# Attention and gated FFN on one core: part of q and k converted by GpSimd's requests, the prologue's steps in another order

## The chip, the cores and the metric

The kernel runs on one core of a Trainium2 chip. The metric is the device time of one execution in microseconds. Before the change it is 343.33 us, the median of three runs (343.06 to 343.74).

## The reference

Inputs are q, k, v of shape 8 x 8 x 576 x 64 (batch, heads, sequence, head dimension) and three weight matrices, all float32.

```
scores = q @ k^T / sqrt(64)                 for each batch and head
scores += slope[h] * (-|i - j|)             slope[h] = 2 ** (-8 (h + 1) / 8)
kept only where 0 <= i - j < 128            (a causal window of 128 positions)
attn = exp(scores - max) / (sum + 1e-9)
x    = (attn @ v), heads side by side       4608 tokens x 512
out  = (gelu(x @ w_gate) * (x @ w_val)) @ w_out      w_gate, w_val 512 x 1536, w_out 1536 x 512
```

## The kernel before

The work goes batch by batch through attention and in groups of 512 tokens through the gated network. Attention of the next batches is woven into the network of the present group, so that TensorE is fed all the time. The schedule is written out by hand: each engine executes its instructions in the order of the program text, and waits are set by the data.

The change touches only the prologue, where nothing can be woven in yet: batch 0's first 384 positions have to go through the whole attention before the first matmul of the network can run.

Heads are handled in pairs, c = 0 to 3, two heads on the two halves of the 128 partitions. The prologue does this:

- **Requests (L650).** q and k of positions 0 to 383 come as float32 in eight requests of two heads each (192 KB, 256 runs of 768 bytes): seven from the queue of SyncE (SP), one (k of pair 0) from ScalarE's. They land in a piece of `wo` and of `qs[1]`, `ks[1]` that is not yet used (`raw`). GpSimd's queue brings, cast to bf16 on the way, the remaining rows 384 to 575 of q and k (`load_runs(0, 1, 0, 8)`, into `vb[1]`), v of batch 0 (`load_v`), and the first columns of the weights (`load_w`, each call one request for gate and one for value).
- **Constants (L654 to L690).** GpSimd makes a ramp `tmpl`; VectorE makes the identity, the distances `dist` with the window in them (`far`), and `slopes`, identity matrices scaled by each head's slope, which add the bias to the scores by a matmul (`biases0`, L284). ScalarE makes `emask`, the exponential of the decays, used for the rows after 384 (`decays`, L684).
- **Cast, transpose, arrange.** `cast` (L693) converts one pair's q or k to bf16 on VectorE or ScalarE; `first` (L708) transposes it on TensorE; `untangle` (L151) copies it from PSUM into `qT`, `kT` in the order of positions.
- **Scores.** `scores0` adds q k^T to the bias in PSUM (L199) and ScalarE takes the exponential (L204, 512 wide, two per pair).
- **Sums and inverses.** `products` (L435) sums the exponentials with a matrix of ones (`sums_first`), two pairs at a time; ScalarE takes the logarithm of the sums (L510) and the exponential of its negative (L511), which is the inverse. A matmul that has to follow another into the same bank waits through a relay on SP (L192).
- **Values.** `products` forms attn @ v, and `scale_first` (L514) multiplies with the inverses into `xT`.
- **Remaining rows.** `rest` (L719) transposes rows 384 to 575 of q and k, after a VectorE copy (L765) has rearranged them; four `untangle` copies follow. `scores0_rest` computes their scores, ScalarE their exponentials (L204, 384 wide, eight of them), VectorE the masks (L207).
- **First network steps.** `gate_val` (L557) multiplies `xT` with the weights; Gelu is on ScalarE (L563, with a table load before the first), the product with the value half on VectorE (L564).

PSUM has eight banks, taken in turn by `bank()`: a bank is free again when its last reader is done. The prologue's order before is the text at L727 to L805.

Of the kernel before, what the change touches and what calls it, by code (L numbers as in the profile page):

```python
# [7 lines left out]
FP32 = mybir.dt.float32  # L8
# [19 lines left out]
def kernel(  # L28
# [10 lines left out]
    nc = tc.nc  # L39
# [583 lines left out]
    def out_last(g):  # L623
        for lo in (0, 256):
# [16 lines left out]
    raw = [[wo[:, 3 + 3 * w:6 + 3 * w, :].rearrange("p a x -> p (a x)").bitcast(FP32),  # L641
            t[1].rearrange("p j x -> p (j x)")[:, 0:1536].bitcast(FP32)]
           for w, t in ((0, qs), (1, ks))]

    pairs0 = [t[0].rearrange("p j x -> p (j x)")[:, 0:1536].rearrange(
        "p (x c y) -> p x c y", x=3, c=4) for t in (qs, ks)]
    pairs1 = wo[:, 9:12, :]
    for h in (0, 2, 4, 6):
        for w, src in ((0, q), (1, k)):
            (nc.scalar if w and h == 0 else nc.sync).dma_start(  # L650
                out=raw[w][h // 4].rearrange("p (h x) -> p h x", h=4)[:, h % 4:h % 4 + 2, :],
                in_=src[0][h:h + 2, 0:384, :].rearrange("h (p r) d -> p h (r d)", r=3))

    nc.gpsimd.iota(tmpl, pattern=[[1, 256]], base=0, channel_multiplier=-1,  # L654
                   allow_small_or_imprecise_dtypes=True)
    nc.gpsimd.memset(ones64, 1.0)
    for t in kT + qT:
        nc.gpsimd.memset(t[:, :, 576:640], 0.0)
    for t in vb:
        nc.gpsimd.memset(t[64:128, 4, :], 0.0)  # L660
    load_runs(0, 1, 0, 8)
    load_v(0, (0, 1, 2))
    load_w(0, 128)
    load_w(128, 256)
    load_v(0, (3, 4))
    load_w(256, 512)

    for h in range(H):
        nc.vector.memset(slope1[:, h:h + 1], -8.0 * 2.0 ** (-8.0 * (h + 1) / H))
    nc.vector.memset(ones8, 0.0)  # L670
    nc.vector.memset(ones8.rearrange("p (h x) -> p h x", x=40)[:, :, 0:8], 1.0)
    nc.vector.tensor_single_scalar(out=ident, in_=tmpl[:, 0:128], scalar=0.0, op=ALU.is_equal)
# [3 lines left out]
    for x in (0, 1):  # L676
        half, to = slice(64 * x, 64 * x + 64), slice(64 * x, 64 * x + 192)
        nc.vector.tensor_tensor(out=dist[half, 0:192], in0=tmpl[half, to], in1=far[half, to], op=ALU.max)
    for to, n in ((192, 192), (384, 128)):
        nc.vector.tensor_copy(out=dist[:, to:to + n], in_=dist[:, 0:n])  # L680
# [11 lines left out]
    def cast(w, c, copy):  # L692
        copy(out=pairs0[w][:, :, c, :].rearrange("p x (i d) -> p x i d", i=2),  # L693
             in_=raw[w][c // 2].rearrange("p (c i x d) -> p c x i d", c=2, i=2, x=3)[:, c % 2])

    made_slopes(0, 4)

# [7 lines left out]
    def first(w, c, copy, ps):  # L705
        ps = ps.bitcast(BF16)
        for x in range(3):
            nc.tensor.transpose(out=ps[:, 128 * x:128 * x + 128], in_=pairs0[w][:, x, c, :],  # L708
                                identity=ident)
        untangle(copy, 0, 0, w, c, c + 1, ps)  # L710

    def rest(copies):
        pss = [bank().bitcast(BF16) for _ in range(2)]
        for c in (0, 2):
            for w, ps in enumerate(pss):
                p = 64 * w
                for n in (c, c + 1):
                    for x in range(3):
                        nc.tensor.transpose(  # L719
                            out=ps[:, 192 * n + 64 * x:192 * n + 64 * x + 64],  # L720
                            in_=pairs1[p:p + 64, x, 128 * n:128 * n + 128],
                            identity=ident[p:p + 64, p:p + 64])
        for c in (0, 2):
            for w, ps in enumerate(pss):
                untangle(copies[w], 0, 1, w, c, c + 2, ps[:, 192 * c:768])

    nc.scalar.preload_act_table_set("natural_log_exp_and_others")  # L727
    held = [bank(), bank()]
    keep_busy(held[0], 2, 128)
    keep_busy(held[0], 60)  # L730
    decays(0, 2)
    cast(0, 0, dve)
    cast(1, 0, act)
    made_slopes(4, 8)
    decays(2, 4)
    first(0, 0, dve, held[0])
    first(1, 0, act, held[1])
    cast(0, 1, dve)
    cast(1, 1, act)
    decays(4, 5)  # L740

    def pair(c, copies, between=None):
        held = [bank(), bank()]
        for w in (0, 1):
            first(w, c, copies[w], held[w])
            if w == 0 and between:
                between()

    cast(0, 2, dve)
    cast(1, 2, dve)  # L750
    scores0((0,), biases0((0,), 4), lambda: pair(1, (dve, act)))
    cast(1, 3, act)
    biases = biases0((1,))
    pair(2, (dve, dve), lambda: cast(0, 3, dve))
    scores0((1,), biases)
    biases = biases0((2,))
    pair(3, (dve, dve))
    scores0((2,), biases)
    scores0((3,), biases0((3,)))
    row(0)  # L760
    sums_a = products(0, sums_first(0))
    for step in zip(*(inverse_first(0, x, sums_a[x]) for x in (0, 1))):
        for do in step:
            do()
    dve(out=pairs1.rearrange("p x (h d) -> p h x d", d=64),  # L765
        in_=vb[1].rearrange("p j x -> p (j x)")[:, 0:1536].rearrange(
            "p (h x d) -> p h x d", h=H, x=3))
# [13 lines left out]
    rest((dve, dve))  # L781
    sums_b = products(0, sums_first(2))
    for x in (0, 1):
        ln, minus = inverse_first(2, x, sums_b[x])
        ln()
        decays(5 + x, 6 + x)
        minus()
    decays(7, 8)
    vals = products(0, values_first(0) + values_first(2, 2))
    for x in (0, 1):  # L790
        for c in (0, 2):
            scale_first(c, x, vals[c + x])
# [31 lines left out]

# [106 lines left out]
```

The softmax here doesn't subtract the row's maximum and nothing guards it: scores larger than these inputs give would overflow.

## Time and profile before

| what | value |
|---|---|
| runs | 343.06, 343.33, 343.74 us |
| span of the profiled execution | 342.5 us (0.8 below the median; what lies around the span is not in the profile) |
| granted TensorE clock | 1.000 over the span |
| TensorE busy | 331.1 us (97%) |
| VectorE, ScalarE, GpSimd busy | 190.8 (56%), 174.4 (51%), 108.1 us (32%) |
| software queue (GpSimd) q0 | 107424 packets, 18.10 MB |
| hardware queues q1 (SP), q10 (ScalarE) | 39104 and 3172 packets |
| first wide matmuls of the network (f = 2) | from 22.82 us on |

Times of the profile count from the start of the span. A line of the chain of waits has a start, a length and the engine and line that the end of the kernel hung on then; a line of the timeline has a start, a busy time, engine, line, operation, tiles, a count, and in brackets the idle time just before and what ended it. "PEld" is the weight load of TensorE, "SPq" the sequencer of SyncE. Beside these views the trace has a record of every DMA packet (queue, start, bytes) and of each request's sixteen partial landings.

### The profile page before, as it was taken

How to read it: one execution, taken by the hardware profiler on the slowest of the kernel's cores; microseconds unless marked ns; L12 is line 12 of the kernel's file. 1: busy time of each engine (PE TensorE's matmuls, PEld its weight loads, DVE VectorE, ACT ScalarE, POOL GpSimd, SP SyncE). 2: the span in 40 equal slices, each digit the busy share in tenths (PEclk: the TensorE clock that was granted, in tenths of full speed). 3: DMA queues.
4: the chain of work that ended last, by engine and by line, in shares of the span. 5: the costliest groups of instructions: out<-in, count | busy, mean ns of one | idle time of the engine just before them, and what ended most of it. 6: DMA issues, size and time to landing. Idle time of an engine off the chain costs nothing.

```text
span 342.5 us, 8046 instructions
## 1 busy us (share of the span) xinstructions
PE 331.1 (97%) x3268; PEld 170.1 (50%) x3310; DVE 190.8 (56%) x331; ACT 174.4 (51%) x339; POOL 108.1 (32%) x147
## 2 busy tenths in 40 slices
PE   7789999999999999999999999999999999999996
PEld 6467655444544454445444554445444544444443
DVE  8679564544599545944595369636773313303420
ACT  6884597536895338443753366344823133224322
POOL 9875663580094095008600680050000000000000
PEclk9999999999999999999999999999999999999999
DMA  8999999999599799979996999587114110020002
GB/s 202 169 196 190 204 164 146 143 188 170 132 145 175 125 190 190 191 165 98 182 183 121 121 181 185 133 107 103 63 40 100 64 64 0 0 94 31 0 31 95
DMA packets 149739, 43.49 MB, mean 127 GB/s; under 512 B 133541, under 2 KB 142661, under 8 KB 149701
## 3 DMA queue, kind: packets, MB, share of 16 engines
q0 software_dynamic: 107424, 18.10, 68.5%
q1 hardware_dynamic: 39104, 18.69, 22.3%
q10 hardware_dynamic: 3172, 6.19, 8.4%
q8 instruction: 26, 0.43, 0.5%
q14 instruction: 13, 0.10, 0.1%
HBM read 43.65 MB, written 9.53 MB: 155 GB/s over the span
## 4 chain that ended last, share of the span: by engine, by line
PE 87%; ACT 8%; DMA 2%; issue 1%; SPq 1%; DVE 0%; ACTq 0%
PE ps L557 54%; PE ps L593 22%; ACT P L204 5%; PE ps L435 4%; DMA ks<-in_k_dram 2%; PE ps L199 2%; PE ps L613 2%; PE ps L251 1%; PE ps L377 1%; ACT osb L598 1%; SPq L650 1%; PE ps L627 1%; PE ps L143 1%; ACT rb L511 0%; ACT rb L510 0%
## 5 line engine op out<-in xcount | busy, mean ns | idle before, releaser
L564 DVE TENSOR_TENSOR hT<-ps,gelu 128x512 bf16<-128x512 f32 (+3 forms) x119 | 74.2, 635 | 91.8 <-PE ps L557 77.8
L563 ACT ACTIVATE gelu<-ps 128x512 bf16<-128x512 f32 (+3 forms) x119 | 65.5, 558 | 103.4 <-PE ps L557 89.5
L557 PE MATMUL ps<-xT,wv 128*128 128x512 bf16 (+3 forms) x472 | 112.9, 359 | 0.4
L557 PE MATMUL ps<-xT,wg 128*128 128x512 bf16 (+3 forms) x461 | 111.7, 359 | 1.2 <-DVE xT L514 0.3
L593 PE MATMUL ps<-wo,hT 128*128 128x512 bf16 x376 | 88.2, 379 | 1.2 <-issue 0.5
L557 PEld LDWEIGHTS <-wv 128*128 128x128 bf16 x476 | 45.2, 98 | 48.6
L557 PEld LDWEIGHTS <-wg 128*128 128x128 bf16 x476 | 44.6, 98 | 48.7 <-issue 0.6
L204 ACT ACTIVATE P<-ps 128x384 bf16<-128x384 f32 (+2 forms) x128 | 55.9, 549 | 15.2 <-PE ps L199 15.0
L593 PEld LDWEIGHTS <-hT 128*128 128x128 bf16 x396 | 37.0, 98 | 44.1
L207 DVE TENSOR_TENSOR P<-P,emask 128x768 bf16<-128x768 bf16 (+1 forms) x60 | 34.4, 588 | 22.1 <-ACT P L204 21.2
L101 POOL DMA_DIRECT2D vb<-in_v_dram x40 | 34.0, 887 | 7.7 <-DMA ks<-in_k_dram 3.3
L598 ACT COPY osb<-ps 128x512 f32<-128x512 f32 x28 | 16.7, 596 | 35.6 <-PE ps L593 34.9
L101 POOL DMA_DIRECT2D qs<-in_q_dram x30 | 25.2, 858 | 5.8 <-DMA wo<-in_moe_w_out_dram 4.0
L882 POOL COPY mark<-hT 1x2 bf16<-1x2 bf16 x4 | 0.7, 174 | 79.6 <-DVE hT L564 79.6
L101 POOL DMA_DIRECT2D ks<-in_k_dram x30 | 25.4, 895 | 0.2 <-DMA qs<-in_q_dram 0.2
L492 DVE TENSOR_TENSOR xT<-ps,rb 128x512 bf16<-128x512 f32 (+3 forms) x29 | 14.3, 563 | 6.9 <-PE ps L435 6.9
L435 PE MATMUL ps<-P,vb 64*64 64x64 bf16 (+2 forms) x752 | 17.8, 221 | 0.3 <-SPq L192 0.2
L435 PEld LDWEIGHTS <-vb 64*64 64x64 bf16 x752 | 14.8, 107 | 4.3 <-issue 2.7
L331 DVE TENSOR_TENSOR T<-P 64x1024 bf16<-64x1024 bf16 (+1 forms) x20 | 15.0, 751 | 0.4
L199 PE MATMUL ps<-qT,kT 64*64 64x192 bf16 (+2 forms) x368 | 11.7, 236 | 0.1
L199 PEld LDWEIGHTS <-kT 64*64 64x64 bf16 x368 | 7.5, 106 | 6.2 <-issue 4.8
L468 DVE TENSOR_TENSOR xT<-ps,rb 128x512 bf16<-128x512 f32 (+1 forms) x10 | 6.4, 638 | 6.8 <-ACT rb L463 6.7
(88 smaller groups left out, 184.4 us busy)
## 6 DMA issues: line engine op xcount, KB each, us to landing
out_dram<-osb SPq DMA_DIRECT2D x35, 256.0 KB
rb<-rd ACTq DMA_DIRECT2D x10, 576.0 KB
vb<-in_v_dram POOLq DMA_DIRECT2D x32, 128.0 KB, 7.2
qs<-in_q_dram POOLq DMA_DIRECT2D x24, 128.0 KB, 4.9
ks<-in_k_dram POOLq DMA_DIRECT2D x24, 128.0 KB, 6.6
wo<-in_moe_w_out_dram POOLq DMA_DIRECT2D x2, 768.0 KB, 14.9
wg<-in_moe_w_gate_dram POOLq DMA_DIRECT2D x5, 256.0 KB, 8.4
wv<-in_moe_w_val_dram POOLq DMA_DIRECT2D x5, 256.0 KB, 9.0
```

Source lines behind the costliest of these rows:

```text
L101: nc.gpsimd.dma_start(out=t[0:n, j, :].rearrange("p (h d) -> p h d", h=H), in_=src[b][:, 128 * j:128 * j + n, :].rearrange("h p d -> p h d"))
L199: nc.tensor.matmul(out=out, lhsT=keys(b, c, m)[half, :], rhs=qT[b % 2][half, c, q0:q0 + n], start=first, stop=True, skip_group_check=not f ...
L204: nc.scalar.activation(out=dst, in_=src, func=AF.Exp, scale=0.125)
L207: nc.vector.tensor_tensor(out=dst, in0=dst, in1=m, op=ALU.mult)
L331: nc.vector.tensor_tensor(out=to[half, :, 2 * n0 + x:2 * n1 + x - 1:2], in0=P[half, :, 3 * n0:3 * n1 - 2:3], in1=P[half, :, 3 * n0 + 1:3 * ...
L435: mm = nc.tensor.matmul(out=out, lhsT=lhsT, rhs=prob(b)[half, c, i, col:col + q1 - q0], start=all(t[2] != u for t in todo[:n]), stop=True, ...
L492: nc.vector.tensor_tensor(out=xT[:, c, at:at + e - a], in0=src, in1=recip[b][:, c, a:e], op=ALU.mult)
L557: nc.tensor.matmul(out=ps, lhsT=w[:, c, 128 * f:128 * (f + 1)], rhs=xT[:, c, t0 + lo:t0 + hi], start=begins, stop=(c == 3), skip_group_che ...
L563: nc.scalar.activation(out=gl[:, 0:n], in_=pg, func=AF.Gelu)
L564: nc.vector.tensor_tensor(out=hid[g][:, f, lo:hi], in0=pv, in1=gl[:, 0:n], op=ALU.mult)
L593: nc.tensor.matmul(out=acc[g], lhsT=hid[g][:, f, 128 * t:128 * (t + 1)], rhs=wo[:, f, :], start=(f == 0), stop=(f == NF - 1))
L598: (nc.vector.tensor_copy if g < B - 2 and t in by_dve.get(g, (0,)) else nc.scalar.copy)(out=osb, in_=acc[g])
```

## The change

Pairs 2 and 3 of q and k are no longer fetched as float32 and cast by VectorE and ScalarE: GpSimd's queue brings them as bf16 (`load_runs(0, 0, 4, 8)`, two requests, ahead of its others) and `transpose_runs` transposes them as they lie. The hardware queues keep the four requests of pairs 0 and 1: q on SP's, k on ScalarE's. The order of the prologue's steps is another one: each pair's transposes stand ahead of the scores of the pair before; more decays are made early; pair 3's scores come after the first sums and the first logarithm; the remaining rows are transposed after the values, straight from where they landed, by twice as many transposes half as wide, and their copies are interleaved with the multiplies of `scale_first`. The first weights come in two requests of 256 columns instead of four of 128.

```diff
-    for h in (0, 2, 4, 6):
+    for h in (0, 2):
         for w, src in ((0, q), (1, k)):
-            (nc.scalar if w and h == 0 else nc.sync).dma_start(
+            (nc.scalar if w else nc.sync).dma_start(
...
     nc.gpsimd.iota(tmpl, pattern=[[1, 256]], base=0, channel_multiplier=-1,
                    allow_small_or_imprecise_dtypes=True)
+    load_runs(0, 0, 4, 8)
     nc.gpsimd.memset(ones64, 1.0)
+    load_v(0, (0, 1, 2))
+    load_runs(0, 1, 0, 8)
+    load_w(0, 256)
+    for t in vb:
+        nc.gpsimd.memset(t[64:128, 4, :], 0.0)
+    load_v(0, (3, 4))
+    load_w(256, 512)
     for t in kT + qT:
         nc.gpsimd.memset(t[:, :, 576:640], 0.0)
-    for t in vb:
-        nc.gpsimd.memset(t[64:128, 4, :], 0.0)
-    load_runs(0, 1, 0, 8)
-    load_v(0, (0, 1, 2))
-    load_w(0, 128)
-    load_w(128, 256)
-    load_v(0, (3, 4))
-    load_w(256, 512)
...
+    def first(w, c, ps):
+        if c < 2:
+            for x in range(3):
+                nc.tensor.transpose(out=ps[:, 128 * x:128 * x + 128], in_=pairs0[w][:, x, c, :],
+                                    identity=ident)
+        else:
+            transpose_runs(0, 0, w, c, ps)
+
+    def rest():
         pss = [bank().bitcast(BF16) for _ in range(2)]
+        for c in range(4):
+            for x in range(3):
+                for i in (0, 1):
+                    for w, ps in enumerate(pss):
+                        p, lo = 64 * w, 192 * c + 64 * x
                         nc.tensor.transpose(
+                            out=ps[64 * i:64 * i + 64, lo:lo + 64],
+                            in_=runs(w, 0, 1)[:, 2 * c + i, 64 * x:64 * x + 64],
                             identity=ident[p:p + 64, p:p + 64])
+        return pss
+
+    def rest_copies(pss, c):
+        for w, ps in enumerate(pss):
+            untangle(dve, 0, 1, w, c, c + 2, ps[:, 192 * c:768])
...
+    def pair(c):
+        if c:
+            pss.append([bank(), bank()])
+        pss[c] = [ps.bitcast(BF16) for ps in pss[c]]
+        for w in (0, 1):
+            first(w, c, pss[c][w])
+
+    def arrange(c, k_by):
+        for w, by in ((0, dve), (1, k_by)):
+            untangle(by, 0, 0, w, c, c + 1, pss[c][w])
+
+    decays(0, 1)
     cast(0, 0, dve)
     cast(1, 0, act)
+    made_slopes(0, 4)
+    decays(1, 2)
+    pair(0)
+    arrange(0, act)
     cast(0, 1, dve)
     cast(1, 1, act)
+    made_slopes(4, 8)
+    decays(2, 3)
+    biases = [biases0((0,), 4)]
+    pair(1)
+    scores0((0,), biases[0])
+    arrange(1, act)
+    decays(3, 6)
+    biases.append(biases0((1,)))
+    pair(2)
+    scores0((1,), biases[1])
+    arrange(2, dve)
+    biases.append(biases0((2,)))
+    pair(3)
+    scores0((2,), biases[2])
+    arrange(3, dve)
     row(0)
     sums_a = products(0, sums_first(0))
-    for step in zip(*(inverse_first(0, x, sums_a[x]) for x in (0, 1))):
-        for do in step:
-            do()
-    dve(out=pairs1.rearrange("p x (h d) -> p h x d", d=64),
-        in_=vb[1].rearrange("p j x -> p (j x)")[:, 0:1536].rearrange(
-            "p (h x d) -> p h x d", h=H, x=3))
+    ln0, minus0 = inverse_first(0, 0, sums_a[0])
+    ln1, minus1 = inverse_first(0, 1, sums_a[1])
+    ln0()
+    scores0((3,), biases0((3,)))
+    minus0()
+    ln1()
+    minus1()
...
-    rest((dve, dve))
     sums_b = products(0, sums_first(2))
     for x in (0, 1):
-        ln, minus = inverse_first(2, x, sums_b[x])
-        ln()
-        decays(5 + x, 6 + x)
-        minus()
-    decays(7, 8)
+        for do in inverse_first(2, x, sums_b[x]):
+            do()
     vals = products(0, values_first(0) + values_first(2, 2))
-    for x in (0, 1):
-        for c in (0, 2):
-            scale_first(c, x, vals[c + x])
+    decays(6, 8)
+    others = rest()
+    scale_first(0, 0, vals[0])
+    rest_copies(others, 0)
+    scale_first(2, 0, vals[2])
+    scale_first(0, 1, vals[1])
+    scale_first(2, 1, vals[3])
+    rest_copies(others, 2)
     scores0_rest((0,), masks)
     gate_val(0, 0, 0, n0, waiting)
     scores0_rest((1,), masks)
```

Besides, VectorE makes `dist` ahead of `slope1` and the identity, and `ones8` is filled later, after the prologue.

## The prediction

> **What bounds the kernel now.** I read the page first, then the chain of waits in order of time, then the timeline of the first 23 us, then the trace's DMA records.
>
> ```profile
> span 342.5 us, 8046 instructions
> ...
> PE 331.1 (97%) x3268; PEld 170.1 (50%) x3310; DVE 190.8 (56%) x331; ACT 174.4 (51%) x339; POOL 108.1 (32%) x147
> ```
>
> TensorE is busy almost throughout. The change touches only the prologue, so the question is when the prologue lets TensorE into its steady part. The chain of waits answers that (start, length, what):
>
> ```profile
> 3.81 6.50 DMA ks<-in_k_dram
> 10.33 0.51 ACT ks L693
> 10.84 2.93 ACT P L204 x6
> 13.78 0.77 ACT rb L510 x2
> 14.54 0.81 ACT rb L511 x2
> 17.69 3.04 ACT P L204 x8
> 20.75 1.28 ACT L563
> 22.82 13.50 PE ps L557 x129
> ```
>
> The last k request (pair 3) is issued at 3.81 and lands 6.50 later. ScalarE then casts it, and everything after is ScalarE back to back: six exponentials, logarithms, inverses, the eight exponentials of the remaining scores, and at 20.75 the table load for Gelu. TensorE enters its steady part at 22.82. After that its idle time adds up to 3.6 us, no gap over 0.2 us, and none ends on a DMA: a shift of the 20.75 goes through to the end one for one.
>
> The timeline shows what else stands in that stretch:
>
> ```profile
> 3.39 0.82 POOL L126 DMA_DIRECT2D vb<-in_q_dram  x1
> ...
> 10.33 0.51 ACT L693 CAST ks<-ks 128x384 bf16<-128x384 f32 x1 [1.61 <-DMA ks<-in_k_dram]
> ...
> 13.21 0.60 PE L719 MATMUL ps<-ident,wo 64*128 64x64 bf16 x24
> ...
> 13.76 0.56 DVE L151 COPY qT<-ps 128x384 bf16<-128x384 bf16 x1 [1.46 <-PE ps L719]
> ...
> 16.43 1.60 DVE L514 TENSOR_TENSOR xT<-ps,rb 128x384 bf16<-128x384 f32 x3 [0.19 <-ACT rb L511]
> ...
> 17.51 3.22 ACT L204 ACTIVATE P<-ps 128x384 bf16<-128x384 f32 x8
> ...
> 20.76 0.56 DVE L207 TENSOR_TENSOR P<-P,emask 128x768 bf16<-128x768 bf16 x1 [0.20 <-ACT P L204]
> ```
>
> ScalarE waits 1.61 us for the last k; this is what the change attacks. And the transposes of the remaining rows (L719) and their four VectorE copies (from 13.76) lie beside the logarithms, before VectorE's four multiplies with the inverses (L514). This is what the change moves.
>
> **Part 1: q, k of pairs 2, 3 through GpSimd.** Four of eight requests leave the hardware queues, with four casts; two software requests of 512 packets of 384 B come, at the head of GpSimd's queue. The iota ends at 1.19, so they are issued from 1.2. Elsewhere in this trace the first packet comes 1.58 to 1.70 us after an issue to an idle software queue (six cases); for the first request of all it took 2.52 us (3.39 to 5.91). So packets come from 2.8 to 3.7, and at strength about 0.4 later.
>
> What they meet there are the four hardware requests that are left, 1024 packets of 768 B. Alone the hardware queues moved 115 to 120 packets per quarter microsecond (3.25 to 4.25). With the software queue beside them, from 6.5 to 8.5, the one hardware queue moved 246 and the software queue 432: 123 and 216 per us, 339 together. The requests show it: the four before landed 0.6 to 0.9 us apart (5.32, 6.21, 6.78, 7.62), the last at 10.31, its sixteen parts spread over 2.05 us (8.26 to 10.31) against 0.6 for the one that landed at 4.71. Now the interleaving falls on the casts that pairs 0 and 1 wait for. By 3.2 the hardware queues have moved some 410 packets, by 4.1 some 840. What is left, 610 or 180, goes at 123 (one hardware queue) to some 230 per us (two against one, if they share evenly); at 200 it takes 3.0 or 0.9 us. With 0.3 us to land and 0.4 to 1.2 us for the slowest part, the k of pair 1 lands between 5.6 and 7.8; I take X = 6.4 (the fourth request of before: 5.32).
>
> The Trainium skill ("DMA: Bandwidth & Descriptors", section on issuing engines not being separate DMA queues) says that requests from different engines interleave on the same sixteen engines and only issue time is saved: against this change as a bandwidth measure. The 339 packets per us above agree. The same page's section on queues, rings and completion order has each engine take turns between its queues by packets; by that alone two hardware queues would keep two thirds of 339, some 226 per us, and X would be about 6.2.
>
> Pairs 2 and 3 then land at L = 7.5 to 9.3: 1024 + 610 packets at 339 per us from 3.2 give 8.0, 1024 + 180 from 4.1 give 7.7, plus landing and spread. Their casts are gone. GpSimd's later requests shift by two places, without a hole, since its queue stays backlogged until 58 us.
>
> **Part 2: the order on ScalarE.** Pair 1's transposes now stand before pair 0's scores on TensorE. From X: cast 0.51, three transposes issued in 0.17, scores 0.41, hops 0.1: pair 0's exponentials at X + 1.2. Then two exponentials (0.477 from start to start), copy 0.375, three decays at 0.264: pair 1's exponentials at X + 3.3 = 9.7. They also need L + 0.7, within this for L up to 9.0. Before they started at 10.75, so the front gains 1.05 us at my X.
>
> **Part 3: sums, logarithms, last scores.** From the start of pair 1's exponentials (call it E): both done 1.08, sums with their relay through SP 1.0: the first logarithm at E + 2.2. Pair 3's bias matmuls (0.43) and scores (0.41) stand behind the sums on TensorE: exponentials at E + 2.75, ScalarE idle some 0.45 in all. They end at E + 3.85. Before, all six ended at 13.78, E + 3.03. The second sums (issued in 0.75) and the values (64 matmuls, 1.11) follow: TensorE is through at E + 5.8.
>
> **Part 4: the remaining rows last.** Now come 48 transposes instead of 24: at 0.02 us each (24 loads took 0.48) half of them 0.45 and 0.19 to drain: E + 6.45. Before, this and the copies lay under the logarithms; now nothing covers them. VectorE copies q and k for pairs 0, 1 (0.475 + 0.556), and the remaining scores of pair 0 (0.43) reach ScalarE at E + 8.1 = 17.8, against 17.51. Then VectorE does three multiplies and two more copies, 3 x 0.475 + 0.475 + 0.556 = 2.46, before the scores of pairs 2, 3 (0.36): E + 10.4 = 20.1. Four exponentials (3 x 0.37 + 0.6): table load at E + 12.1 = 21.8, against 20.75. The chain from E was 10.0 and becomes 12.1: 2.1 lost, 1.05 gained, **+1.05 us**. The mask multiplies end 0.7 after, as now (21.32).
>
> **Part 5, nothing each.** The rearranging copy of L765 (0.55) goes from VectorE, where it filled a gap. SP keeps two requests; its relays, the first at 12.7, meet none. The banks taken again are free by then; the remaining rows' two wait for pair 3's exponentials, which are done at E + 3.97. Weights: four requests of 256 B packets (about 690 per us) become two of 512 B (381 to 384 per us), 2.97 to 2.68 us of queue; the first landing moves from 14.82, 15.54 to about L + 6.0 and L + 7.3, at most 16.6, needed at 17.7. Were it late, the lag would pass through TensorE to the scores. The pads of kT, qT now come behind GpSimd's weights, at some 13 us, needed from 17. ones8's two memsets (0.2) go into VectorE gaps of 1.4 us near 37. ScalarE's second issue (0.51) delays its table load to 3.1, and its first input arrives at 4.1.
>
> **How it stands to the runs.** The sum is made in the span of 342.5; the median of the runs is 343.33, 0.8 more. 343.33 + 1.05 = 344.4. About 0.2%, 0.69 us here, is what measurement can tell from no change.
>
> **Rivals.** *A, mild interleaving.* Software packets come late and the slowest part lags little: X near 5.6. Then ScalarE's own order holds the front (cast behind the copy of pair 0's k), E = 9.0, table load 21.1: +0.35, 343.7. For it: the 2.52 us of the first issue. Against: the spread of 2.05 us. *B, heavy interleaving.* Packets at 2.8, hardware at 123 per us or a lagging part: X = 7.8, E = 11.1, +2.45, 345.8. For it: the six idle-queue issues; against: two hardware queues take turns instead of one. *C, faster.* ScalarE's own work decides: without the waits of parts 3 and 4 its instructions from E take some 9.5 us. If the transposes and copies of part 4 hide under the inverses (values early, banks released one by one), the chain from E is 10.3 and at E = 9.2 the table load comes at 19.5: -1.2, 342.1. It decides where the chain from E is under 10.0 + (10.75 - E). Against it: VectorE's eight instructions after the values take 3.9 us in a row, and TensorE's order is fixed. *D*, that the change reaches nothing because the wait is elsewhere, falls: the 1.61 us wait is on the chain.
>
> **Chances.** Forecast (X from 6.0 to 7.0, 343.9 to 345.1) 0.45, A 0.25, B 0.22, C 0.08. Slower by over 0.2%: B and nearly all of the forecast, 0.65; within: A and the rest, 0.27; faster: C, 0.08. The range leaves out most of C and the far end of B: 343.0 to 346.0.
>
> **What would show it.** Right: exponentials of pair 1 starting at 9 to 10.5; remaining transposes after the values; a wait of ScalarE before the first 384-wide exponential, ended by TensorE behind VectorE's copies; VectorE without a gap from the values to the second copies; table load near 21.8. Wrong: the k of pair 1 landing by 5.4 or after 8; pair 1's exponentials waiting for L; 384-wide exponentials without gaps; a TensorE wait for weights.

## The result, and the profile after

The changed kernel takes 346.25 us (median of 20 runs, 345.80 to 346.82), beside 343.87 us for the kernel before (20 runs, 343.06 to 346.36). The ratio is 1.0063, interval 1.0050 to 1.0076: slower by about 2.2 to 2.4 us. The forecast was 344.4 with a range to 346.0. The direction was right, the size too small.

The page of the changed kernel, first lines: its span, its busy times, and the queue that will matter below (packets, MB, share of the DMA engines).

```profile
span 344.0 us, 8138 instructions
...
PE 334.4 (97%) x3346; PEld 169.7 (49%) x3346; DVE 186.7 (54%) x327; ACT 174.6 (51%) x338; POOL 108.5 (32%) x147
...
q8 instruction: 26, 0.43, 0.5%
```

In every profiled execution here the time of the run is 1.7 to 1.9 us above its span (345.86 for this one). So the profile before, with its span of 342.5, was a run of some 344.2 us, 0.3 to 0.4 above the median of its kernel, and this one is at the fast end of its own (345.80 to 346.82). The two spans, 1.5 us apart, understate the difference.

The chain of waits of the changed kernel, from the remaining rows to the first wide matmuls (start, length, what):

```profile
15.36 0.51 PE ps L712 x38
15.87 0.55 DVE qT L151
16.42 0.47 DVE kT L151
16.89 1.39 DVE xT L514 x3
18.28 0.46 DVE qT L151
18.74 0.48 DVE kT L151
...
19.62 0.49 issue
20.11 0.32 PE ps L199 x3
20.43 1.63 ACT P L204 x4
...
22.07 1.28 ACT L563
```

`L712` is the transposes of the remaining rows, and `issue` is time in which the engine waited for nothing that the profile shows. Where ScalarE ran back to back before, the chain now goes through TensorE's transposes of the remaining rows, then through VectorE for 3.4 us (copies, multiplies, copies), and then through 0.49 us of "issue". The table load for Gelu starts at 22.07 against 20.75. The timeline shows the same place from each engine:

```profile
9.10 2.29 ACT L204 ACTIVATE P<-ps 128x512 bf16<-128x512 f32 x4
...
12.18 1.08 ACT L204 ACTIVATE P<-ps 128x512 bf16<-128x512 f32 x2 [0.41 <-PE ps L199]
...
17.35 0.87 ACT L204 ACTIVATE P<-ps 128x384 bf16<-128x384 f32 x2 [0.37 <-PE ps L199]
...
20.42 1.64 ACT L204 ACTIVATE P<-ps 128x384 bf16<-128x384 f32 x4 [1.14 <-PE ps L199]
...
15.16 0.56 DVE L514 TENSOR_TENSOR xT<-ps,rb 128x384 bf16<-128x384 f32 x1 [4.36 <-PE ps L435]
...
19.27 0.35 PE L199 MATMUL ps<-qT,kT 64*64 64x64 bf16 x9
20.11 0.44 PE L199 MATMUL ps<-qT,kT 64*64 64x192 bf16 x15 [0.49 <-issue]
```

The marks that are compared, in the kernel before (pair 1's exponentials, the scores of pairs 2 and 3, the table load):

```profile
10.75 3.03 ACT L204 ACTIVATE P<-ps 128x512 bf16<-128x512 f32 x6
...
18.53 0.53 PE L199 MATMUL ps<-qT,kT 64*64 64x64 bf16 x24
...
20.75 1.28 ACT L563 ACT_TABLE_LOAD   x1
```

Pair 1's exponentials (E) start at 9.10, against 10.75: the front did gain. The four exponentials of pairs 2 and 3 wait 1.14 us for scores that TensorE began at 19.27. It stopped after nine of 24 and began the rest at 20.11. The next three belong to pair 2 like the nine, with the same copies and the same banks, so neither can have been missing. VectorE was idle for 4.36 us before its chain.

The time follows one mark: in the 13 profiled runs whose time is on record (all but the profile before), the time less the start of the table load is 323.5 to 324.0 us, whether that load starts at 19.87 or at 24.06. So every experiment is read by E, by the table load, and by the chain between the two. Each ratio is to the runs of the kernel before in the same series, whose medians go from 343.71 to 344.21 us:

```
kernel                               E      table load   chain    median us   ratio to before
before                             10.75      20.75      10.00     343.87      1
before, longer warm-up             10.53      20.55      10.02     344.10      0.9990
before, shorter warm-up            10.20      20.70      10.50     345.70      1.0035
before, remaining rows late        10.13      21.21      11.08     344.70      1.0011
changed                             9.10      22.07      12.97     346.25      1.0063
changed, repeated                   9.79      22.86      13.07     346.37      1.0055
changed, narrow weights             9.49      22.56      13.07     346.33      1.0056
changed, small first request        9.27      22.35      13.08     346.26      1.0066
changed, remaining rows early       9.66      22.09      12.43     345.46      1.0019
changed, shorter warm-up            9.50      21.73      12.23     345.49      1.0028
changed, both                       9.12      20.13      11.01     343.98      1.0004
  and decays in ScalarE's waits     9.30      20.66      11.36     344.21      1.0003
  and pair 1's scores first         8.68      19.87      11.19     343.73      0.9987
changed, longer warm-up            10.52      24.06      13.54     346.37      1.0073
```

E moves by up to 0.7 us between runs of one kernel, the chain by 0.1. For E the means are therefore used: 10.40 over the four kernels with the requests of before, 9.41 over the first four of the changed kind.

### The profile page after: what moved, and what is told of

The parts are those of the page before. It is cut to its first block, busy times and chain, and to the rows that moved or that the text cites. A ratio compares the mean times of both kernels' runs of the same rounds, so it can differ in the third digit from the quotient of the medians.

```text
span 344.0 us, 8138 instructions
## 1 busy us (share of the span) xinstructions
PE 334.4 (97%) x3346; PEld 169.7 (49%) x3346; DVE 186.7 (54%) x327; ACT 174.6 (51%) x338; POOL 108.5 (32%) x147
## 4 chain that ended last, share of the span: by engine, by line
PE 93%; ACT 3%; DVE 2%; DMA 1%; issue 0%; SPq 0%; ACTq 0%
PE ps L557 54%; PE ps L593 25%; PE ps L435 5%; PE ps L199 2%; PE ps L251 2%; PE ps L613 2%; ACT P L204 1%; DMA wo<-in_q_dram 1%; PE ps L377 1%; PE ps L143 1%; PE ps L627 1%; DVE qT L151 0%; DVE xT L514 0%; ACT L563 0%; ACT rb L462 0%
## 5 line engine op out<-in xcount | busy, mean ns | idle before, releaser
L557 PE MATMUL ps<-xT,wg 128*128 128x512 bf16 (+3 forms) x476 | 113.5, 359 | 0.3 <-DVE hT L564 0.2
L593 PE MATMUL ps<-wo,hT 128*128 128x512 bf16 x396 | 90.4, 379 | 0.0
```

Source lines behind the costliest of these rows:

```text
L557: nc.tensor.matmul(out=ps, lhsT=w[:, c, 128 * f:128 * (f + 1)], rhs=xT[:, c, t0 + lo:t0 + hi], start=begins, stop=(c == 3), skip_group_che ...
L593: nc.tensor.matmul(out=acc[g], lhsT=hid[g][:, f, 128 * t:128 * (t + 1)], rhs=wo[:, f, :], start=(f == 0), stop=(f == NF - 1))
```

## The experiments

Three things could have lengthened the chain: the remaining rows, moved behind the values; the wider weight requests; and the stop marked "issue", which may be the loading of TensorE's instructions. The first runs take the first two.

**The changed kernel again**, and **the weights of the first 256 columns in four requests**:

> The changed kernel once more, with a second profile. Its first profile put 1.55 us on the span (342.5 to 344.0) where the runs put 2.2 to 2.4, and it showed TensorE idle for 0.49 us amid the remaining scores of pair 2 (20.11), for nothing that the profile names. If that gap belongs to the program (its code), it is there again at the same instruction; if it is chance, it is gone and the span is 343.3 to 343.6. Time against before: +2.0 to +2.5 us. If the part outside the span is the program's, time less span is again some 0.9 us more than for before.

```diff
-    load_w(0, 256)
+    load_w(0, 128)
+    load_w(128, 256)
```

> The changed kernel with the first weights in four requests of 128 columns again. All theories: 0.3 us later landing of the weights after them, no change of the table load (22.07), time within 0.2 us of the changed kernel. Were the wider requests what stalls TensorE's first network steps, this one would be 0.3 us or more faster.

Measured: 346.37 us (1.0055, interval 1.0024 to 1.0087) and 346.33 us (1.0056, 1.0037 to 1.0076), chain 13.07 in both. The width of the weight requests has no share in the loss that the runs could tell.

**The remaining rows early.** In the changed kernel, the transposes and copies of the remaining rows go back in front of the second sums:

```diff
+    others = rest()
+    rest_copies(others, 0)
+    rest_copies(others, 2)
     sums_b = products(0, sums_first(2))
...
-    others = rest()
     scale_first(0, 0, vals[0])
-    rest_copies(others, 0)
     scale_first(2, 0, vals[2])
     scale_first(0, 1, vals[1])
     scale_first(2, 1, vals[3])
-    rest_copies(others, 2)
```

> The changed kernel with the remaining rows moved back: their 48 transposes ahead of the second sums, their four VectorE copies ahead of the multiplies. Theory 'cover' (the loss is that these transposes and copies lost their cover under the logarithms): no gap before or among the eight 384-wide exponentials, which start at 16.9 to 17.4; table load at 20.1 to 20.6 against 22.07; time 1.5 to 2.0 us under the changed kernel, 0 to 0.6 us from before. Rival 'front' (the requests and the new order of the scores cost the time): the table load comes no earlier than 21.5 and the time stays 1.3 us or more above before. Rival 'outside' (the loss is in code and start, not in this chain): table load as in 'cover', but the time stays 0.7 us or more above before.

Measured: 345.46 us (1.0019, 0.9987 to 1.0050). The gain of 0.9 us was smaller than the loss of 2.2 to 2.4 us, and the table load (22.09) stayed where the rival 'front' had put it. But the timeline shows another reason than that rival's:

```profile
20.43 1.64 ACT L204 ACTIVATE P<-ps 128x384 bf16<-128x384 f32 x4 [1.37 <-PE ps L199]
...
18.79 0.35 PE L199 MATMUL ps<-qT,kT 64*64 64x64 bf16 x9
20.13 0.44 PE L199 MATMUL ps<-qT,kT 64*64 64x192 bf16 x15 [0.98 <-issue]
```

The scores of pairs 2 and 3 begin at 18.79, half a microsecond earlier, and stop again after nine matmuls, until 20.13, almost the moment at which the changed kernel went on (20.11). What the early rows gain, this stop takes.

**The remaining rows late, alone, in the kernel before.** Its transposes go behind the values, and the copies between the multiplies, as in the change:

```diff
-    rest((dve, dve))
     sums_b = products(0, sums_first(2))
...
+    others = rest()
     scale_first(0, 0, vals[0])
+    rest_copies(others, 0)
     scale_first(2, 0, vals[2])
     scale_first(0, 1, vals[1])
     scale_first(2, 1, vals[3])
+    rest_copies(others, 2)
```

> The kernel before with this one part of the change: the transposes of the remaining rows after the values, their copies among the multiplies. Theory 'cover': the scores of pair 1 and of pairs 2, 3 of the remaining rows come later, gaps among the 384-wide exponentials, table load at 21.3 to 21.6 against 20.75, time +0.5 to +0.9 us. Rival 'front': within 0.2 us of before.

Measured: 344.70 us (1.0011, 0.9991 to 1.0032), chain 11.08 against 10.00. ScalarE gets the waits of the changed kernel:

```profile
17.24 0.87 ACT L204 ACTIVATE P<-ps 128x384 bf16<-128x384 f32 x2 [0.16 <-PE ps L199]
18.30 0.87 ACT L204 ACTIVATE P<-ps 128x384 bf16<-128x384 f32 x2 [0.19 <-PE ps L199]
19.56 1.64 ACT L204 ACTIVATE P<-ps 128x384 bf16<-128x384 f32 x4 [0.39 <-PE ps L199]
```

These waits sum to 0.74 us. The wait before pairs 2 and 3 is 0.39, not 1.14: with half as many transposes ahead, there is no stop amid the scores here. The move alone lengthens the chain by 1.1 us; the times put it at 0.4 (by ratio) to 0.8 us (by median), with an interval that includes no change.

**The stop follows a count, not an instruction.** Every matmul has one weight load. The records of the loads are complete (3346 in the changed kernel); of the matmuls some are missing in some traces. In each row below TensorE stopped when 352 weight loads had been issued (224 in one row), whatever came next. By matmul records that is about 350 and 222, the numbers that the expectations and the text below use. Each time a 16384-byte packet of the queue "instruction" had begun 2.2 to 2.5 us before TensorE went on:

```
kernel                          packet starts   loads   goes on    what stood still
changed                            17.88         352     20.11     remaining scores of pair 2
changed, repeated                  18.55         352     20.90     remaining scores of pair 2
changed, remaining rows early      17.89         352     20.13     remaining scores of pair 2
changed, both                      18.49         352     20.86     gate and value matmuls
before, shorter warm-up            13.86         224     16.17     values
```

From 224 to 352 are 128 loads with 128 matmuls, one packet if an instruction has 16384 / 256 = 64 bytes. That length is also the one that the Trainium skill gives ("Perfetto Trace Analysis", the 4-stage abstract model). The number of packets goes with the same step: the kernels with 3310 to 3394 loads have 26, and the one with 3280 (before, shorter warm-up), which ends short of the next count of this row (224 + 24 x 128 = 3296), has 25. The skill's page "Trainium Architecture — The Big Picture" (the software stack) has the instruction streams brought to the engines when the program is loaded; here 26 such packets came while the kernel ran.

The packet itself does not start at a fixed count: the second one of each trace starts when 240 to 339 loads have been issued. So TensorE stands still only where it reaches the count sooner than some 2.2 us after that start. In the changed kernel it did so after 1.4 us (19.32). The kernel before reached the same count 3.7 us after the start of its packet (17.66 and 21.38), and did not stop there.

The changed kernel has 36 more matmuls before the remaining scores of pair 2: 24 more transposes of the remaining rows and 12 more of pairs 2 and 3. That puts count 350 among these scores. The warm-up (62 matmuls of zeros, no result) can move the count without touching any other step: four kernels change it alone or with the rows.

```diff
-    keep_busy(pss[0][0], 2, 128)
-    keep_busy(pss[0][0], 60)
+    keep_busy(pss[0][0], 32, 128)
```

> The changed kernel with 30 fewer TensorE instruction pairs in its warm-up: 32 matmuls of 128 columns in place of 2 of 128 and 60 of 64, the same columns and 3.4 us. In all four profiles of this order TensorE stops at its matmul number 350 (amid the remaining scores of pair 2) and goes on 2.23 to 2.35 us after the start of a 16384-byte packet of the instruction queue. Theory 'code' (this stop is TensorE's instructions not yet being loaded): the stop goes from the scores of pair 2 and stands some 30 matmuls later or is hidden; the 384-wide exponentials of pair 2 start 0.7 to 0.8 us earlier against those of pair 0; time 0.4 to 0.9 us under the changed kernel (346.3). Rival 'data' (the stop is a wait for a bank or a copy): it stays at the same place of the program and the time is unchanged.

This with the remaining rows early as above:

> The remaining rows early, as in the run with that name, and the shorter warm-up code. There the scores of pair 2 were ready for issue at 18.9 and TensorE stopped to 20.13. Theory 'code': the eight 384-wide exponentials run without a gap, table load about 3.0 us after the first of them (20.4 to 20.6 at a first one of 17.45), time 1.3 to 1.6 us under that run: 343.9 to 344.2, about before. Rival 'data': as that run, 345.5.

In the kernel before, 90 matmuls of warm-up, and 32, in place of 62:

```diff
     keep_busy(held[0], 2, 128)
-    keep_busy(held[0], 60)
+    keep_busy(held[0], 88, 44)
```

```diff
-    keep_busy(held[0], 2, 128)
-    keep_busy(held[0], 60)
+    keep_busy(held[0], 32, 128)
```

> The kernel before with 28 more TensorE instruction pairs in its warm-up (88 matmuls of 44 columns for 60 of 64, the same columns), which puts the matmul number 350 into the remaining scores of pairs 2 or 3. Theory 'code': a stop of TensorE there or just behind, up to 1 us of table load and of time (+0.3 to +1.0 us). Rival 'data': within 0.2 us of before.

> The kernel before with the 32 wide warm-up matmuls: a second profile of the prologue of before, and a control for the two above. Both theories: within 0.3 us of before. In the profile used for the forecast the last k landed at 10.31 and the span was 342.5, while most timed runs of before since have spans of 341.6 to 342.0; if the late landing was chance, the last k lands near 9.7 here and pair 1's exponentials start near 10.1.

Measured in the changed kernel with the shorter warm-up: 345.49 us (1.0028, 1.0009 to 1.0046), 0.8 us less with everything else in place. Its timeline has all 24 scores in one run, and the wait is down from 1.14 to 0.39:

```profile
19.67 0.54 PE L199 MATMUL ps<-qT,kT 64*64 64x64 bf16 x24
...
20.07 1.64 ACT L204 ACTIVATE P<-ps 128x384 bf16<-128x384 f32 x4 [0.39 <-PE ps L199]
```

With both: 343.98 us (1.0004, 0.9982 to 1.0026), the loss is gone. ScalarE's eight exponentials of the remaining rows again run without a gap, and the stop, still at count 350, falls beside the table load, where nobody waits for TensorE:

```profile
16.91 3.21 ACT L204 ACTIVATE P<-ps 128x384 bf16<-128x384 f32 x8
20.13 1.28 ACT L563 ACT_TABLE_LOAD   x1
...
20.86 0.24 PE L557 MATMUL ps<-xT,wv 128*128 128x192 bf16 x1 [0.91 <-issue]
```

In the kernel before the longer warm-up changed nothing (344.10 us, 0.9990, 0.9967 to 1.0013). The loss of 0.3 to 1.0 us that the code theory expected did not come; by the time alone the rival was right. The count did fall among the scores of pairs 2 and 3, but the packet had begun at 16.28, 2.0 us ahead of them, so the stop was only 0.23 us long (24 scores in 0.76 us, 0.53 before), and ScalarE's exponentials covered it:

```profile
18.31 0.76 PE L199 MATMUL ps<-qT,kT 64*64 64x64 bf16 x24
...
17.30 3.23 ACT L204 ACTIVATE P<-ps 128x384 bf16<-128x384 f32 x8
```

The shorter warm-up, less code, made the kernel before slower, which neither theory had expected: 345.70 us (1.0035, 1.0009 to 1.0061). The count of 222 there falls among the values, ahead of the multiplies:

```profile
14.01 1.06 PE L435 MATMUL ps<-P,vb 64*64 64x64 bf16 x51
16.17 0.36 PE L435 MATMUL ps<-P,vb 64*64 64x128 bf16 x9 [1.11 <-issue]
```

The chain of this last kernel grew by 0.5 us, which is less than its 1.2 to 1.5 us (by ratio and by median). The rest goes with the granted clock: the four of its ten runs at 1.000, the profiled one among them, took 344.43 to 344.94 us, some 0.5 above the 344.13 that is the median of the 26 runs before at 0.998 or more, and the other six had 0.989 to 0.995, as 9 of 35 runs before had. Whether the shorter warm-up brings on the lower clock is not shown. At the full clock, then, the same edit gains 0.8 us in one kernel and loses 0.5 in the other: not the warm-up's length matters, but the place of the count.

**More code in the changed kernel** (48 matmuls more, 108 of 36 columns in place of 60), so that count 350 falls at a wait that is there anyway:

```diff
-    keep_busy(pss[0][0], 60)
+    keep_busy(pss[0][0], 108, 36)
```

> The changed kernel with 48 more matmuls in the warm-up (108 of 36 columns in place of 60 of 64), so more code but no more work. TensorE's 350th matmul then is not among the remaining scores of pair 2 (where it stood 0.5 us with 0.7 between starts) but at the first matmul of the remaining scores, where it already waited 1.19 us for the copy of kT. Theory that TensorE stops while its code is loaded, at a fixed count of its matmuls: the stop hides behind that wait, the scores of pair 2 run through, and the time falls from 346.3 by 0.4 to 0.9, unless the count of 222, which then falls near the sums at 12 us, stops it there: then the stop is seen at that matmul and the time stays. Rival, that the shorter warm-up helped for its time or its clock and not for its count: the stop stays at the same instruction (pair 2's scores) and the time at 346.1 to 346.6.

```profile
9.77 0.36 PE L143 MATMUL ps<-ident,ks 128*64 128x128 bf16 x6 [1.68 <-DMA ks<-in_k_dram]
...
14.91 1.09 ACT L204 ACTIVATE P<-ps 128x512 bf16<-128x512 f32 x2 [0.95 <-PE ps L199]
...
19.68 0.36 PE L199 MATMUL ps<-qT,kT 64*64 64x64 bf16 x12 [1.18 <-DVE kT L151]
...
22.00 0.53 PE L199 MATMUL ps<-qT,kT 64*64 64x64 bf16 x24
...
24.06 1.28 ACT L563 ACT_TABLE_LOAD   x1
```

Measured: 346.37 us (1.0073, 1.0048 to 1.0099): no gain. Behind the front the code theory held: the stop left pair 2's scores (24 in one run), the count was reached where TensorE waited 1.18 us anyway, and from pair 3's exponentials to the table load it took 9.15 us (14.91 to 24.06), the same as with the shorter warm-up (12.58 to 21.73), against 9.89 to 10.00 in the four kernels with the stop. The loss came back in the front, by a way that neither theory had named. An instruction packet came already at 7.41 and took 0.98 us, and the last two of the sixteen parts of k of pairs 2 and 3 landed at 8.28 and 9.73, against 7.21 and 7.49 in the changed kernel, whose packet came at 9.67, after them. TensorE waited 1.68 us and E came at 10.52. That the packet held the DMA engine of the last part is inferred, since no record names a packet's engine: behind it the next request's last part lags as much (10.57 after 9.13), and in the changed kernel, with its packet at 9.67, this lag goes from 0.30 us in the request landed at 10.07 to 0.95 in the next. It is not all of it, for q of these pairs was late too (7.69 against 6.34), in part before the packet came. The profiled run was one of the slowest of its six (347.54; 345.70 to 347.81), so the size of this in a usual run is not settled.

**A small request first in GpSimd's queue**:

```diff
+    nc.gpsimd.dma_start(out=wo[0:16, 9, 0:64], in_=q[0, 0, 0:16, :])
     nc.gpsimd.iota(tmpl, pattern=[[1, 256]], base=0, channel_multiplier=-1,
```

> The changed kernel with one request more at the head of GpSimd's queue, a small one (16 rows of 64), ahead of the iota, so that the queue has moved something before the loads of pairs 2 and 3 are asked for. Theory that the queue's first request of a program is late by itself (2.8 to 3.0 us from issue to first packet here, 1.6 us where the queue had just been used): the packets of pairs 2 and 3 begin 1 us earlier, at 3.2 to 3.6, among the hardware queues' packets, q and k of pair 1 land later than 5.5, at 5.8 to 6.4 as the prediction had it, and the pairs 2 and 3 land about 0.5 earlier. Rival, that each request of this queue takes 2.8 us here because the hardware queues have the engines first: the packets begin 2.8 us after the issue again, and pair 1 lands at 5.4 to 5.6. The time should move by less than 0.5 us either way.

Measured: 346.26 us (1.0066, 1.0041 to 1.0092). The test could not tell the two apart as planned: the small request was issued at 1.28, hardly before the 1.35 of the first one in the changed kernel, and the first packet came at 4.11, 2.83 later. The request behind it, issued at 2.30, had its first packet at 4.15, after 1.85 us, so 2.8 us is not what each request takes here. The k of pair 1 landed at 5.42. Nor is such a delay peculiar to the first request of the program: every trace has one later case of an idle queue, near 120 us, in which the first packet came 2.7 to 5.2 us after the issue (119.91 to 125.07 before), each time 0.1 to 0.9 us ahead of the last packet of a large load on ScalarE's queue. Nearly all other issues to the idle queue took 1.6 us (at most 2.2). That the packets of ScalarE's queue hold it up is not tested; that the first packet comes too late to hold up pair 1 is seen in all kernels of the changed kind.

**What was left: ScalarE's decays, and the order in front of E.** First the decays out of ScalarE's path, on top of "both":

```diff
-    decays(0, 1)
+    decays(0, 3)
...
-    decays(1, 2)
+    decays(3, 4)
...
-    decays(2, 3)
+    decays(4, 6)
...
-    decays(3, 6)
...
     ln0()
+    decays(6, 7)
...
-    decays(6, 8)
+    decays(7, 8)
```

> The version with early remaining rows and the shorter warm-up (343.98 us, 1.0004 of before), with four of the six later decay rows (0.30 us of ScalarE each) moved from between the copy of k of pair 1 and the exponentials of pair 1 into ScalarE's waits: two more at 3.5, before the cast of k of pair 0 (which there waited 0.77 us for its landing), one at 6.4 ahead of pair 0's exponentials (which waited 0.52), one between the first logarithm and pair 3's exponentials (which waited 0.41). Theory that ScalarE's own queue is what is left of the loss (from pair 0's exponentials at 7.0 to the table load at 20.1 it stood only 0.41 us): E falls from 9.12 to about 8.75 and the table load from 20.13 to 19.2 to 19.7, the time by 0.4 to 0.9, to 343.1 to 343.6, under before by 0.2 to 0.3%. Rival, that TensorE's sums and the landing of v set the order behind E: E falls as far, but the table load stays within 0.2 of 20.1 and the time within 0.2 of 344.0.

Measured: 344.21 us (1.0003, 0.9985 to 1.0021): nothing gained. E did not fall as both sides had expected (9.30, from 9.12), and the table load (20.66) was later than either had put it. ScalarE now waits instead:

```profile
9.30 1.08 ACT L204 ACTIVATE P<-ps 128x512 bf16<-128x512 f32 x2 [0.51 <-PE ps L199]
...
8.31 0.36 PE L143 MATMUL ps<-ident,ks 128*64 128x128 bf16 x6 [0.21 <-DMA ks<-in_k_dram]
...
12.93 0.57 PE L712 MATMUL ps<-ident,vb 64*64 64x64 bf16 x47 [0.58 <-DMA vb<-in_k_dram]
```

The decays had filled a wait. Pair 1's scores stand behind pair 2's transposes on TensorE, and those behind the landing of k of pairs 2 and 3, in this run at 8.27. So pair 1's scores went ahead of them, and VectorE copies pair 1's k, which on ScalarE came behind pair 0's exponentials:

```diff
-    decays(4, 6)
+    decays(4, 5)
...
-    arrange(1, act)
+    arrange(1, dve)
     biases.append(biases0((1,)))
-    pair(2)
     scores0((1,), biases[1])
+    decays(5, 8)
+    pair(2)
...
-    decays(6, 7)
...
-    decays(7, 8)
```

> The version with early remaining rows, the shorter warm-up and the decay rows in ScalarE's waits (344.21 us), with pair 1's scores put ahead of pair 2's transposes on TensorE, k of pair 1 copied by VectorE and not by ScalarE behind pair 0's exponentials, and the last three decay rows behind pair 1's exponentials. There pair 1's exponentials (E) waited for TensorE, which stood for the landing of k of pairs 2 and 3 (8.27). Theory that this landing and ScalarE's copy are what holds the front: pair 1's scores are done near 8.0, E follows pair 0's exponentials without a wait at 8.2 to 8.5 (from 9.30), pair 2's exponentials come at 9.9 to 10.4 (from 10.63), and the table load at 19.2 to 20.0 (from 20.66), the time 0.5 to 1.2 lower, 343.0 to 343.7. Rival, that what stands behind E (the sums before pair 3's scores, the landing of v, the multiplies) sets the table load: E comes as early, but pair 3's exponentials stay within 0.3 of 12.3, the table load within 0.3 of 20.4, and the time within 0.4 of 344.1.

```profile
7.67 2.10 ACT L204 ACTIVATE P<-ps 128x512 bf16<-128x512 f32 x4 [0.52 <-PE ps L199]
...
12.19 1.09 ACT L204 ACTIVATE P<-ps 128x512 bf16<-128x512 f32 x2 [0.22 <-PE ps L199]
...
19.87 1.28 ACT L563 ACT_TABLE_LOAD   x1
...
20.87 0.24 PE L557 MATMUL ps<-xT,wv 128*128 128x192 bf16 x1 [1.19 <-issue]
```

Measured: 343.73 us (0.9987, 0.9961 to 1.0014). Each side is half right. Pair 1's exponentials follow pair 0's without a wait, at 8.68 and not at 8.2 to 8.5 because pair 0's came later here (7.67), and the table load is the earliest of all, within the theory's 19.2 to 20.0. But pair 3's exponentials stay at 12.19, as the rival said: they stand behind the first sums. Part of the gain may go again, though no run shows it: TensorE's stop at count 350 now ends at 20.87, only 0.3 us before the first Gelu (21.16), and the time less the table load is 323.87, against 323.59 and 323.62 in the two versions before it. The version is level with the kernel before, not measurably better.

## Why the prediction was wrong in size

- **Part 1, interleaving.** X, the k of pair 1, was forecast at 6.4 with bounds of 5.6 to 7.8; it landed at 5.48 (5.25 to 5.58 in the other kernels of the changed kind), below the bound. The software queue's first packet came 3.0 us after its issue, not in 1.6 to 2.5, when the hardware requests were nearly done. The rule on interleaving hardly applied, because there was little left to interleave with. The reading behind this term was too narrow: of the six later issues to an idle queue in the trace before, five took 1.58 to 1.62 us and one, at 119.91, took 5.16. L was right: 7.48 to 8.41 for k, forecast 7.5 to 9.3 (9.73 with the longer warm-up alone).
- **Part 2, the front.** E was forecast at X + 3.3 = 9.7 and came at 9.10, 9.27, 9.49 and 9.79. The gain of the means, 10.40 to 9.41, is 1.0 us; the forecast had 1.05. This agreement is in part luck, for the path was another one. From pair 0's exponentials to pair 1's it took 2.1 us in seven kernels, as forecast (3.3 less 1.2). But pair 0's came at 7.00 to 7.69 and not at X + 1.2 = 6.7, and the chain of the changed kernel does not touch X there. It comes from the landing of q of pair 0, through VectorE's casts and copies:

```profile
0.75 3.28 DMA wo<-in_q_dram
...
4.05 0.43 DVE qs L694
4.48 0.59 DVE wo L682
5.07 0.47 DVE qT L151
5.54 0.43 DVE qs L694
...
6.02 0.59 PE ps L700 x6
6.61 0.40 PE ps L199 x10
7.01 1.08 ACT P L204 x2
```

In four others it comes from TensorE's warm-up. ScalarE's cast of the k of pair 1, which had landed at 5.48, began at 5.70, behind the copy of pair 0's. E scatters with the time at which TensorE reaches full speed: the granted clock is 1.0 from 3.9 us on in the changed kernel (E 9.10) and from 5.5, 6.0, 6.7, 6.8 and 7.0 on in five of its variants (9.12, 9.27, 9.49, 9.50, 9.66). In the repeated one (6.1 and 9.79) the cast of q took 0.90 us besides, against 0.43.

- **Parts 3 and 4, the chain.** Forecast 10.0 to 12.1. Without the stop it was 12.23 (shorter warm-up): the working of the two parts, waits and VectorE's order included, was right to 0.13 us, with misses on the way that partly cancel: pair 3's exponentials came at E + 3.08, forecast E + 2.75, pair 0's remaining ones at E + 8.25, forecast E + 8.1.
- **The term that was missing.** With the stop the chain was 13.0: Part 4 entered the scores of pairs 2 and 3 at their bare 0.36 us; from their first matmul to the exponentials it took 1.15 us (19.27 to 20.42), and 0.40 where the count had been moved (19.67 to 20.07). The 24 more transposes of the remaining rows and the 12 more of pairs 2 and 3 were costed by their time, not by where they put TensorE's count. This is the step that failed, and it is worth 0.8 to 1.1 us in the changed kernel (medians 346.3 to 345.49, ratios 1.0055 to 1.0066 against 1.0028). The kernel before reaches the same count too late after its packet to stop at all.
- **Part 5** held: the weights cost nothing that shows in either width.
- **How it stands to the runs.** The 0.8 us between span and median were read as a fixed distance; it is 1.7 to 1.9. That does not shift the difference, but the median of three runs that was added to (343.33) was itself 0.5 below that of the twenty (343.87), and 0.5 us of the miss of 1.85 (344.4 to 346.25) is this.
- **The sum.** Chain 10.0 to 13.05, front 10.40 to 9.41: +2.1 us, beside the 2.2 to 2.4 measured. By parts, from the changed kernel and by medians (the kernel before had 343.86 in the series with the first edits and 344.21 in that with the shorter warm-up): shorter warm-up -0.8, then early rows -1.5; the other way round, early rows -0.9, then shorter warm-up -1.5. Each edit seems to hide part of the other, since the scores of pairs 2 and 3 start when both VectorE's copies and TensorE's code are there.
- **The rivals.** A's front came true without A's result. Heavy interleaving (B) did not happen; its time, 345.8, was nearly right for another reason. C asked that the transposes and copies hide under the inverses: with the rows early they do, and without the stop the chain is 11.0 and not C's 10.3, which the front's 1.0 just pays for.

## What to carry to other kernels

When a change adds small matmuls, count instructions as well as time: TensorE here stood for up to 1.2 us at counts 128 matmuls apart, in stretches of small ones, where it came to the count within some 2 us of the start of the packet, and that costs whatever waits for the matmul at that count. A step that only looks cheap because it lies beside other work has to be costed again where it is put: 24 transposes and four copies were free beside the logarithms and lengthened the chain by 1.1 us behind the values. Compare medians of many runs, and read single profiles by a mark such as the table load, since the front alone moved by 0.7 us between runs.

## What was not expected of the hardware

- TensorE stops, it seems for its own code: up to 1.19 us at counts 128 matmuls apart, in stretches of matmuls of 64 to 192 columns, going on 2.2 to 2.5 us after the start of a 16384-byte packet. That the stop is the loading of code is inferred from this packet, the fixed count, the number of packets and the kernels in which the count was moved; no record names it.
- Such a packet took about 0.97 us in these prologues (0.89 to 1.32), and in one run the last part of a request under way with it landed 1.45 us after the fifteenth; that both used one engine is inferred.
- The first packet of GpSimd's queue came 2.8 to 3.1 us after the first issue of the program in the kernels of the changed kind, where the same queue, idle later on, mostly took 1.6 us, but 2.7 to 5.2 us beside a large load on ScalarE's queue.
